# Where two query chunks are scaled, and where two keys' maxima and exponentials stand, in the first stage of an attention and Fourier-mixing kernel

## The chip, the cores and the metric

The kernel runs on one core of one Trainium2 chip. The time is device microseconds of one execution. Five engines work on their own instruction queues, each in program order: PE (TensorE: matrix products, and transposes done as products with an identity), DVE (VectorE), ACT (ScalarE), POOL (GpSimd) and SP (SyncE, which here only issues transfers). They wait for each other by semaphores. PE writes its results to an accumulator memory that DVE and ACT read.

## The reference

Eight batches of 576 tokens, eight heads of 64. The keys' softmax runs over the tokens, the queries' softmax over the 64 channels of a head:

```
q_s = exp(q - max(q, axis=-1));  q_s = q_s / (sum(q_s, axis=-1) + 1e-9)
k_s = exp(k - max(k, axis=2));   k_s = k_s / (sum(k_s, axis=2) + 1e-9)
kv  = einsum('bhsd,bhse->bhde', k_s, v)
x   = einsum('bhsd,bhde->bhse', q_s, kv)          # then (B, S, H*D)
u   = x + real(fft(fft(x, axis=1), axis=2))
un  = (u - mean(u)) / sqrt(var(u) + 1e-6)
out = u + relu(un @ w_ch1) @ w_ch2
```

A query row's softmax denominator is one number per token and head, and the product with kv is linear in the row. So a row may be divided before the product or the result after it.

## The kernel before

**Tiling.** Of a batch's 576 tokens 512 are worked on as four chunks of 128, named by (c, u) and below q00, q01, q10 and q11; the 64 others of two batches share one chunk (the "t" rows). The products x of a chunk land in a tile of its own, x00 to x11; c picks the half of a tile, u the tile. A batch has four key groups of 128 channels (two heads each).

**The stage in question** is the first batch, ahead of the first up-projection (`plain`, L876). The feed-forward part of batch after batch comes behind it and fills PE; the attention of the next batch is laid among those products. Only the first batch has no feed-forward to hide behind. In it, in order:

- *Keys.* `k_exp` (maximum, exponential with a running sum, reciprocal), `k_turn` (transposes on PE, copied to `ks` by ACT and, the fifth piece, DVE), `k_times_v` (product, scaled into the block-diagonal `kvr`).
- *Queries.* `q_exp` takes the maximum per head (L604, DVE), eight exponentials (L606, ACT), the sum, the added epsilon and the reciprocal (L608 to L610, DVE) and multiplies the chunk by it in place (L611, DVE). `q_turn` transposes it (L617, PE) and copies the result to `qT` (L624, ACT). `q_times_kv` multiplies by kvr (L649, PE) into an accumulator `acc` and copies it to x (L651, ACT). `acc` has three buffers, the transposes' `tr` has two, qT has two. `t_times_kv` does the same for the shared rows (L659, L665; copies L662 and L666).
- *Second batch's keys.* Their loads are at hand early. `second_keys` returns `maxima` and two lists of steps. `maxima` waits by a gate for their data and takes all four maxima (L468, DVE); a second gate, written behind x11, holds the first exponentials back until x is there. A gate is a one-row bit operation on DVE that reads one tile and rewrites another with its own value, so that what reads the second must wait for the first. `exps` does two exponentials (L475, ACT, with running sums) and two small DVE operations (L482, L483). The first two keys are exponentiated behind x, and transposed and multiplied between the folds and the Fourier blocks; the other two behind the first of the two mixes.
- *Transform.* `at_first` adds and subtracts the halves of x and folds columns (L688, L694, L703, L709, L710, all DVE); two of the column folds feed a product into scrap (`warm`, L206, PE), which writes nothing that is used. At its end a `wait_for` ties the first piece of weights (`convert(0)`: L351 and L356 on ACT, L352 and L353 on DVE, L357 on POOL) to the folds. Then five `block` steps: three products (L742, L745, PE) and three copies (L748, L751, L753, ACT) to Z.
- *Mixes.* `mix_own` twice: products (`second`, L766, L769), a copy to `sn` (L773, ACT), two combinations (L780, DVE), additions to x (L787, L788, DVE). Behind the first sn stands a gate on the second pair of maxima (L494).
- *Norm.* Statistics (L815, L816, DVE), root (L819, ACT), reciprocal (L820), the normalized rows (L832, DVE, order 0, 2, 1, 3), their transposes (L846, PE), the copies to `unT` (L850, ACT); with `unT` complete L876 begins. An unused `root` operation in `exps` (L481) has ACT load the table of the square root ahead of L819.

**Order.** The steps are listed by hand (L1098): `one` is the first batch's attention, `two` its folds, five blocks and two mixes, `some` and `others` the second batch's key steps. A scheduler then places the instructions of neighbouring steps on each engine; on the chip each engine runs its list in that order.

Of the kernel before, what the change touches and what calls it, by code (L numbers as in the profile page):

```python
# [40 lines left out]
F32 = mybir.dt.float32  # L41
I32, U32 = mybir.dt.int32, mybir.dt.uint32
ACT = mybir.ActivationFunctionType
ALU = mybir.AluOpType
AX = mybir.AxisListType

P = 128
B, H, S, DH = 8, 8, 576, 64
D = H * DH
FF = 4 * D  # L50
NR = H // 2
NC = 5
HD = D // 2
NN = HD + 1
# [43 lines left out]
def pipelined(items, stages):  # L98


    def step(t):
        for s in range(len(stages) - 1, -1, -1):
            if 0 <= t - s < len(items):
                stages[s](items[t - s])

    return [lambda t=t: step(t) for t in range(len(items) + len(stages) - 1)]
# [8 lines left out]
def interleaved(t):  # L115

    return t.rearrange("p (a q) -> p q a", a=2)


def paired(t):  # L120
    return t.rearrange("p (q a) -> p q a", a=2)


class _Block:
# [63 lines left out]
    def turned(self):  # L188
        t = self.ps.tile([P, 4, P], F32, tag="tr", name="tr", bufs=2)
        return t  # L190
# [264 lines left out]
    def second_keys(self):  # L455


        nc, V = self.nc, self.nc.vector
        items = [("k", 1, r) for r in range(NR)]
        m, rec = (self.small.tile([P, NR], F32, tag=n, name=n, bufs=1) for n in ("km1", "krec1"))  # L460

        self.km1 = m

        def maxima():
            self.gate(self.at_start[2][0][:, 1, :], self.second_at[0][0:1, ::S])
            for it in items:
                self.k_load(it)
                V.reduce_max(m[:, it[2]:it[2] + 1], self.live[it][0], axis=AX.X, negate=True)  # L468

            self.gate(self.xpart(0, 1, 1), m[0:1, 0:2])  # L470

        def exps(some):
            for it in some:
                k, i = self.live[it][0], slice(it[2], it[2] + 1)
                nc.scalar.activation(k, k, ACT.Exp, bias=m[:, i], accum_out=rec[:, i])  # L475
                self.live[it].append(rec[:, i])
            i = slice(some[0][2], some[-1][2] + 1)
            if some[-1] == items[-1]:

                t = self.small.tile([P, 1], F32, tag="root", name="root", bufs=1)  # L480
                nc.scalar.activation(t[:], rec[:, NR - 1:], ACT.Sqrt)  # L481
            V.tensor_scalar(out=rec[:, i], in0=rec[:, i], scalar1=ATT_EPS, scalar2=None, op0=ALU.add)  # L482
            V.reciprocal(rec[:, i], rec[:, i])  # L483

        turned = lambda some: pipelined(some, [self.k_turn, self.k_times_v])
        return maxima, [lambda: exps(items[:2])] + turned(items[:2]), [lambda: exps(items[2:])] + turned(items[2:])

    def gate(self, t, raw):
# [109 lines left out]
    def q_exp(self, it):  # L598
        nc, V = self.nc, self.nc.vector
        q = self.live[it][0]  # L600
        heads = q.rearrange("p (h d) -> p h d", h=H)
        spread = lambda t: t[:].unsqueeze(2).to_broadcast([P, H, DH])
        m = self.small.tile([P, H], F32, tag="qm", name="qm", bufs=3)
        V.reduce_max(m[:], heads, axis=AX.X, negate=True)  # L604
        for h in range(H):
            nc.scalar.activation(heads[:, h, :], heads[:, h, :], ACT.Exp, bias=m[:, h:h + 1])  # L606
        rec = self.small.tile([P, H], F32, tag="qrec", name="qrec", bufs=3)
        V.reduce_sum(rec[:], heads, axis=AX.X)  # L608
        V.tensor_scalar(out=rec[:], in0=rec[:], scalar1=ATT_EPS, scalar2=None, op0=ALU.add)
        V.reciprocal(rec[:], rec[:])  # L610
        V.tensor_tensor(out=heads, in0=heads, in1=spread(rec), op=ALU.mult)  # L611

    def turned_q(self, it):
        q = self.live.pop(it)[0]
        pt = self.turned()
        for r in range(NR):
            self.nc.tensor.transpose(pt[:, r, :], q[:, r * P:(r + 1) * P], self.ident[:])  # L617
        return pt

    def q_turn(self, it):  # L620
        _, b, c, u = it
        pt = self.turned_q(it)
        qT = self.work.tile([P, NR, P], F32, tag="qT", name="qT", bufs=2)
        self.nc.scalar.copy(qT[:], pt[:] if c == u else pt[:, :, ::-1])  # L624
        self.live[it] = qT

    def t_turn(self, it):
        pt = self.turned_q(it)
        self.tq = self.work.tile([P, NR, P], F32, tag="tq", name="tq", bufs=1)
        self.nc.scalar.copy(self.tq[:], pt[:])  # L630

# [11 lines left out]

    def q_times_kv(self, it):
        nc, (_, b, c, u) = self.nc, it
        qT = self.live.pop(it)
        px = self.acc((P, D))
        for r in range(NR):
            nc.tensor.matmul(px[:, r * P:(r + 1) * P], lhsT=qT[:, r, :], rhs=self.kvr[b % 2][:, r, :], start=True,  # L649
                             stop=True)  # L650
        nc.scalar.copy(self.xpart(b, c, u), px)  # L651

    def t_times_kv(self, b):
        nc, V = self.nc, self.nc.vector
# [20 lines left out]
    def transform(self, b):  # L675


        nc, V, G = self.nc, self.nc.vector, self.nc.gpsimd
        Z = self.work.tile([P, KT, HD], F32, tag="Z", name="Z", bufs=1)
        self.Z[b] = Z  # L680
        x = {(c, u): self.xpart(b, c, u) for c in range(2) for u in range(2)}
        eo = {}
# [34 lines left out]
        def at_first():  # L717

            for some in ((2, 3), (0, 1)):
                for f in (tokens_folded, columns_folded, by_frequency, columns_again):  # L720
                    f(some)

            self.wait_for(eo[1][:, NN:], [self.raws[0]])

        def block(k):

# [32 lines left out]
    def second(self, z, zr, add):  # L759

        nc, V = self.nc, self.nc.vector
        pm = self.acc((P, D))
        cd, n = self.cd, 0
        for k, at, size in ((1, 0, QD), (0, QD, QD + 1), (3, NN, QD - 1), (2, NN + QD - 1, QD)):
            rows = QD - 1 if k == 3 else P
            nc.tensor.matmul(pm[:, at:at + size], lhsT=z(k)[0:rows], rhs=cd[0:rows, at:at + size], start=True,  # L766
                             stop=(k != 0))
            if k == 0:
                nc.tensor.matmul(pm[:, at:at + size], lhsT=zr, rhs=cd[:, D:], start=False, stop=True)  # L769

        sn = self.sn[self.turns % 2]
        self.turns += 1
        nc.scalar.copy(paired(sn[:, 0:HD]), interleaved(pm[:, HD:]))  # L773
        if self.turns == 1:

            self.gate(sn[:], self.km1[0:1, 2:4])
        two = self.halves()
        a = interleaved(pm[:, 0:2 * (QD + 1)])[:, 0:QD, :]
        for i, op in enumerate((ALU.subtract, ALU.add)):
            V.tensor_tensor(out=paired(two[:, i * NN + 1:(i + 1) * NN]), in0=a, in1=paired(sn[:, 1:NN]), op=op)  # L780
        V.tensor_copy(two[:, ::NN], pm[:, QD:QD + 1].to_broadcast([P, 2]))
        add(two[:, 0:NN], two[:, NN:])
# [260 lines left out]
def kernel(ctx: ExitStack, tc: tile.TileContext, q, kT, v, w1, w2, ft,  # L1043
# [4 lines left out]
    def front(b, loads=None):  # L1048

        first = blk.attention(b, loads)  # L1050
        steps = late(lambda: blk.transform(b), (6, 9, 10)[min(b, 2)])
        mixes = [lambda c=c: blk.mix_own(b, c) for c in range(2)]
        if b % 2:

            mixes.insert(0 if b == B - 1 else 2, lambda: blk.mix_shared(b // 2))
        return first, steps + mixes

    def late(make, n):

        box = []  # L1060

        def run(i):
            if not box:
                box.extend(make())
            box[i]()

        return [lambda i=i: run(i) for i in range(n)]
# [3 lines left out]
    def norm(g):  # L1071
        def make():
            nexts[g], steps = blk.norm(g)
            return steps
        return late(make, 7)
# [19 lines left out]
    free = blk.hold()  # L1095
    one, two = front(0)
    maxima, some, others = blk.second_keys()
    for step in one + [maxima] + some[:1] + two[:1] + some[1:] + two[1:-1] + others[:1] + two[-1:] + others[1:] + norm(0):  # L1098
        step()

    groups = [*range(B - 1), B, B - 1]
    for order, g in enumerate(groups):
        loads = [] if g == 0 else None
        one, two = front(order + 1, loads) if order + 1 < B else (blk.later, [])
# [101 lines left out]
```

## Time and profile before

| what | us |
|---|---|
| median of 4 runs | 1129.68 (1128.59 to 1133.9) |
| the profiled execution | 1127.47 |
| its span, first to last instruction | 1125.6 |
| PE busy | 1091.7 |
| DVE, ACT, POOL busy | 542.7, 404.7, 333.9 |
| first up-projection product (L876) starts | 62.11 |

The span leaves out what lies around the instructions, 1.87 us in this execution. A row of the timeline has the start, the duration, the engine, the line of the kernel, the operation, what it writes and reads, and in brackets how long the engine was idle before it and whom it waited for. An "x2" row merges neighbouring instructions of one kind; the time from one start to the next can be shorter than the duration, since instructions of an engine overlap at their ends. Rows of PE's and of DVE's busy time count an engine as busy while an instruction is in it.

### The profile page before, as it was taken

Reading aid. Unit: us, or ns where it says so; the run is one execution under the profiler, and the core shown is the slowest. Engines: PE = TensorE matmul, PEld = TensorE weight load, DVE = VectorE, ACT = ScalarE, POOL = GpSimd, SP = SyncE. Lnnn points to the kernel's source line nnn. Section 1 sums busy time; section 2 is a strip of 40 time slices with the busy share of each in tenths; the row PEclk is TensorE's granted clock in tenths of the full one; section 3 lists DMA queues with packets and bytes.
Section 4 is the critical chain, followed back from the end, with each engine's and each line's share of the span. In section 5 each row is a group of like instructions: output and inputs, shape, how many; then the busy total and the mean of one; then the engine's idle time right before and its main releaser. Section 6 shows DMA issues by size and latency. Waiting matters only on the chain.

```text
span 1125.6 us, 14593 instructions
## 1 busy us (share of the span) xinstructions
PE 1091.7 (97%) x5440; PEld 915.7 (81%) x5440; DVE 542.7 (48%) x1117; ACT 404.7 (36%) x975; POOL 333.9 (30%) x304
## 2 busy tenths in 40 slices
PE   5799999999999999999999999999999999999997
PEld 5644456888888888898889888888889888888886
DVE  6784795478334733484434643683334252103301
ACT  6695424264224413361325232532333152201200
POOL 2064671244022510333023402351035203402320
PEclk9999999999999999999999999999999999999999
DMA  9566685454266424663455436543453443434451
GB/s 311 171 219 190 242 314 193 148 213 169 103 192 200 175 108 145 202 221 116 153 178 188 151 126 204 195 156 112 149 184 150 143 147 140 187 140 157 152 187 56
DMA packets 92582, 193.79 MB, mean 172 GB/s; under 512 B 23121, under 2 KB 59729, under 8 KB 85345
## 3 DMA queue, kind: packets, MB, share of 16 engines
q1 hardware_dynamic: 90712, 191.82, 49.6%
q10 hardware_dynamic: 1800, 1.05, 0.3%
q8 instruction: 43, 0.70, 0.3%
q14 instruction: 27, 0.21, 0.1%
HBM read 168.72 MB, written 28.31 MB: 175 GB/s over the span
## 4 chain that ended last, share of the span: by engine, by line
PE 85%; DVE 1%; POOL 1%; ACT 1%; issue 1%; ACTq 0%; POOLq 0%
PE bb L946 15%; PE bb L984 15%; PE ba L946 10%; PE bc L984 10%; PE bc L946 10%; PE ba L984 10%; PE acc L567 2%; PE acc L649 2%; PE bc L885 2%; PE acc L766 1%; PE acc L742 1%; PE acc L745 1%; PE tr L846 1%; PE tr L617 1%; PE tr L553 1%
## 5 line engine op out<-in xcount | busy, mean ns | idle before, releaser
L946 PE MATMUL bb<-unT,big 128*128 128x256 f32 x768 | 187.4, 381 | 0.0
L984 PE MATMUL bb<-big 128*128 128x256 f32 x768 | 172.1, 379 | 0.0
L946 PEld LDWEIGHTS bb<-unT,big 128*128 128x128 f32 x768 | 142.8, 190 | 23.6 <-DVE u L914 2.6
L984 PEld LDWEIGHTS bb<-big 128*128 128x128 f32 x768 | 145.4, 190 | 20.3
L363 POOL TENSOR_TENSOR big<-big 128x512 f32<-128x512 f32 (+1 forms) x38 | 46.2, 1216 | 306.9 <-ACT big L958 306.0
L958 ACT ACTIVATE big<-big 128x512 f32<-128x512 f32 x96 | 60.3, 629 | 182.6 <-DVE big L957 182.1
L946 PE MATMUL bc<-unT,big 128*128 128x256 f32 x512 | 125.4, 379 | 0.0
L946 PE MATMUL ba<-unT,big 128*128 128x256 f32 x512 | 123.6, 379 | 0.2 <-ACT unT L850 0.2
L984 PE MATMUL bc<-big 128*128 128x256 f32 x512 | 116.0, 379 | 0.5 <-DVE x L1001 0.5
L984 PE MATMUL ba<-big 128*128 128x256 f32 x512 | 114.8, 379 | 0.0
L918 DVE TENSOR_TENSOR u<-bb,s 128x512 f32<-128x512 f32 x40 | 27.6, 691 | 178.5 <-PE bb L984 120.8
L984 PEld LDWEIGHTS bc<-big 128*128 128x128 f32 x512 | 96.1, 190 | 14.3 <-DVE x L1001 0.9
L984 PEld LDWEIGHTS ba<-big 128*128 128x128 f32 x512 | 95.7, 190 | 12.1
L946 PEld LDWEIGHTS bc<-unT,big 128*128 128x128 f32 x512 | 95.1, 190 | 12.7
L946 PEld LDWEIGHTS ba<-unT,big 128*128 128x128 f32 x512 | 95.1, 190 | 12.2 <-ACT unT L850 0.5
L371 POOL TENSOR_TENSOR unT<-unT 128x512 f32<-128x512 f32 x8 | 14.2, 1773 | 182.4 <-DVE unT L370 182.4
L606 ACT ACTIVATE q<-q,qm 128x64 f32<-128x64 f32 x240 | 61.9, 340 | 5.7 <-DVE qm L604 5.4
L914 DVE TENSOR_TENSOR u<-bb,s 128x512 f32<-128x512 f32 x40 | 27.6, 691 | 72.9 <-PE bb L946 38.7
L957 DVE TENSOR_TENSOR big<-bc,u 128x512 f32<-128x512 f32 x64 | 44.1, 690 | 22.8 <-PE bc L946 21.7
L996 POOL TENSOR_TENSOR x<-x,u 128x512 f32<-128x512 f32 x14 | 17.7, 1266 | 113.9 <-DVE u L918 101.7
L850 ACT COPY unT<-tr 128x512 f32<-128x512 f32 x36 | 20.7, 586 | 79.4 <-PE tr L846 78.8
L957 DVE TENSOR_TENSOR big<-bb,s 128x512 f32<-128x512 f32 x32 | 22.1, 691 | 55.8 <-PE bb L946 55.8
(253 smaller groups left out, 1651.6 us busy)
## 6 DMA issues: line engine op xcount, KB each, us to landing
big<-w1s SPq DMA_DIRECT2D x64, 896.0 KB
big<-w2s SPq DMA_DIRECT2D x56, 1024.0 KB
big<-in_w_dram SPq DMA_DIRECT2D x21, 512.0 KB
q<-in_q_dram SPq DMA_DIRECT2D x27, 256.0 KB
k<-in_kT_dram SPq DMA_DIRECT2D x24, 288.0 KB
v<-in_v_dram SPq DMA_DIRECT2D x24, 256.0 KB
words<-in_w_dram SPq DMA_DIRECT2D x8, 512.0 KB
mirror<-x SPq DMA_DIRECT2D x14, 256.0 KB
```

The source lines that it names most:

```text
L363: e1.tensor_tensor(out=to(4), in0=at(2), in1=at(3), op=ALU.add)
L567: nc.tensor.matmul(pk, lhsT=ks[:, c, :], rhs=v[:, c, :], start=(c == 0), stop=(c == NC - 1))
L606: nc.scalar.activation(heads[:, h, :], heads[:, h, :], ACT.Exp, bias=m[:, h:h + 1])
L649: nc.tensor.matmul(px[:, r * P:(r + 1) * P], lhsT=qT[:, r, :], rhs=self.kvr[b % 2][:, r, :], start=True, stop=True)
L850: nc.scalar.copy(unT[:, u:u + 3:2, :, cols], pt[:].rearrange("p (a k) t -> p a k t", a=2))
L885: nc.tensor.matmul(po[:], lhsT=h[:, f, i * P:(i + 1) * P], rhs=self.w2sb[:, f, :], start=(f == 0), stop=(f == NF - 1))
L914: V.tensor_tensor(out=temp("u2"), in0=box["bb"][:], in1=box["s1"][:], op=ALU.add)
L918: V.tensor_tensor(out=temp("u3"), in0=box["bb"][:], in1=box["s1"][:], op=ALU.add)
L946: nc.tensor.matmul(bank()[:, i, :], lhsT=w[:, WA_AT[m], k * P:(k + 1) * P], rhs=unT[:, B_AT[m], k, :], start=first and i == 0 and k == 0, ...
L957: V.tensor_tensor(out=hp(i), in0=bank[:], in1=u[:], op=ALU.add)
L958: nc.scalar.activation(hp(i), hp(i), ACT.Relu)
L984: nc.tensor.matmul(bank()[:, i, :], lhsT=h[p][:, A_AT[m], i * P:(i + 1) * P], rhs=w[:, p, :], start=first and i == 0 and p == 0, stop=p == ...
```

## The change

Four edits. The denominators of q00 and q11 of the first batch are no longer multiplied into the chunk ahead of the transposes; they are kept, and DVE multiplies them in where it writes x00 and x11 out of the accumulator, in place of ACT's copy. The maxima of the third and fourth key of the second batch move out of `maxima` to the start of the second `exps`, behind a gate on the last fold; the wait that ties the first piece of weights to the folds now ties it to these maxima. The second `exps` step moves from between the two mixes to between the folds and the Z blocks. The gate behind the first sn goes, and the unused square root moves behind the second sn.

```diff
         def maxima():
             self.gate(self.at_start[2][0][:, 1, :], self.second_at[0][0:1, ::S])
             for it in items:
                 self.k_load(it)
+            for it in items[:2]:
                 V.reduce_max(m[:, it[2]:it[2] + 1], self.live[it][0], axis=AX.X, negate=True)
 
             self.gate(self.xpart(0, 1, 1), m[0:1, 0:2])
 
         def exps(some):
+            if some[-1] == items[-1]:
+
+                self.gate(self.folded, self.second_at[0][0:1, 2 * S::S])
+                for it in some:
+                    V.reduce_max(m[:, it[2]:it[2] + 1], self.live[it][0], axis=AX.X, negate=True)
+
+                self.wait_for(m[:, 2:4], [self.raws[0]])
             for it in some:
                 k, i = self.live[it][0], slice(it[2], it[2] + 1)
                 nc.scalar.activation(k, k, ACT.Exp, bias=m[:, i], accum_out=rec[:, i])
                 self.live[it].append(rec[:, i])
             i = slice(some[0][2], some[-1][2] + 1)
-            if some[-1] == items[-1]:
-
-                t = self.small.tile([P, 1], F32, tag="root", name="root", bufs=1)
-                nc.scalar.activation(t[:], rec[:, NR - 1:], ACT.Sqrt)
...
-        rec = self.small.tile([P, H], F32, tag="qrec", name="qrec", bufs=3)
+        rec = self.small.tile([P, H], F32, tag="qrec", name="qrec", bufs=4)
         V.reduce_sum(rec[:], heads, axis=AX.X)
         V.tensor_scalar(out=rec[:], in0=rec[:], scalar1=ATT_EPS, scalar2=None, op0=ALU.add)
         V.reciprocal(rec[:], rec[:])
+        if it[:2] == ("q", 0) and it[2] == it[3]:
+
+
+            self.live[it].append(spread(rec))
+            return
         V.tensor_tensor(out=heads, in0=heads, in1=spread(rec), op=ALU.mult)
...
-        qT = self.live.pop(it)
+        qT, *rec = self.live.pop(it)
         px = self.acc((P, D))
...
-        nc.scalar.copy(self.xpart(b, c, u), px)
+        x = self.xpart(b, c, u)
+        if rec:
+            heads = lambda a: a.rearrange("p (h d) -> p h d", h=H)
+            nc.vector.tensor_tensor(out=heads(x), in0=heads(px), in1=rec[0], op=ALU.mult)
+            return
+        nc.scalar.copy(x, px)
...
-            self.wait_for(eo[1][:, NN:], [self.raws[0]])
+            self.folded = eo[1][:, NN:]
...
-        if self.turns == 1:
-
-            self.gate(sn[:], self.km1[0:1, 2:4])
+        if self.turns == 2:
+
+            t = self.small.tile([P, 1], F32, tag="root", name="root", bufs=1)
+            nc.scalar.activation(t[:], sn[:, 0:1], ACT.Sqrt, scale=0.0)
...
-    for step in one + [maxima] + some[:1] + two[:1] + some[1:] + two[1:-1] + others[:1] + two[-1:] + others[1:] + norm(0):
+    for step in one + [maxima] + some[:1] + two[:1] + some[1:] + others[:1] + two[1:] + others[1:] + norm(0):
         step()
```

## The prediction

> **What bounds it now.** First the busy shares and the last chain on the page:
> ```profile
> PE 1091.7 (97%) x5440; PEld 915.7 (81%) x5440; DVE 542.7 (48%) x1117; ACT 404.7 (36%) x975; POOL 333.9 (30%) x304
> PE 85%; DVE 1%; POOL 1%; ACT 1%; issue 1%; ACTq 0%; POOLq 0%
> ```
> PE is the bound. The timeline of PE shows it full from the first up-projection (L876, 62.11 us) on, with one stall of 4.13 us at 139.3 to 143.4. The change touches only what lies ahead of 62.11; instruction orders after that are the same. So the forecast is the shift of that 62.11. The chain view names no piece before 126.92, so I follow the start in the timeline (start, duration, engine, idle before). First where the x rows are made:
> ```profile
> 28.40 0.69 DVE L611 TENSOR_TENSOR big<-big,qrec 128x512 f32<-128x512 f32 x1
> 29.24 0.63 PE L617 MATMUL tr<-ident,big 128*128 128x128 f32 x4
> 29.96 0.59 ACT L624 COPY qT<-tr 128x512 f32<-128x512 f32 x1 [1.46 <-PE tr L617]
> 30.44 0.58 ACT L666 COPY xs<-acc 64x512 f32<-64x512 f32 x1
> 30.92 1.07 ACT L651 COPY x<-acc 128x512 f32<-128x512 f32 x2
> 31.07 2.05 PE L649 MATMUL acc<-kvr,qT 128*128 128x128 f32 x16 [1.20 <-ACT xs L666]
> 32.02 0.69 DVE L688 TENSOR_TENSOR eo<-x 128x512 f32<-128x512 f32 x1
> 33.78 0.15 DVE L494 SCALAR_TENSOR_TENSOR km<-x,km 1x2 int32<-1x2 int32 x1 [0.61 <-ACT x L651]
> ```
> One thread: scaling q11, its transposes, two ACT copies, two products, x11, the gate, the next fold at 33.85. Then the end of the stage:
> ```profile
> 45.93 0.37 ACT L748 COPY Z<-acc 128x256 f32<-128x256 f32 x1 [0.43 <-PE acc L745]
> 48.35 0.37 ACT L773 COPY sn<-acc 128x256 f32<-128x256 f32 x1 [0.87 <-PE acc L766]
> 50.47 0.35 ACT L773 COPY sn<-acc 128x256 f32<-128x256 f32 x1
> 52.24 0.57 ACT L554 COPY ks<-tr 128x512 f32<-128x512 f32 x1
> 55.75 2.22 PE L567 MATMUL acc<-big,ks 128*128 128x128 f32 x10 [0.46 <-ACT ks L554]
> 56.34 0.17 DVE L820 RECIPROCAL std<-std 128x2 f32<-128x2 f32 x1 [0.45 <-ACT std L819]
> 58.67 0.59 ACT L850 COPY unT<-tr 128x512 f32<-128x512 f32 x1
> ```
> ACT waits for PE in the Z blocks; behind sn it is late itself: the second sn follows two exponentials, then a table load (50.83, 1.28), then ks. PE is slow in one stretch (PE busy, ..., clock):
> ```profile
> 34.10:37.50 3.40, 1.96 (x11) 1.29 (x9) 3.40 (x11) 1.80 (x5) 0.00 (x0) 1.00 1.10 348
> 50.70:54.10 3.40, 1.24 (x11) 1.24 (x12) 3.40 (x13) 2.34 (x5) 0.00 (x0) 1.00 0.02 5
> 54.10:57.50 3.40, 2.94 (x15) 2.54 (x14) 2.92 (x12) 2.06 (x6) 0.00 (x0) 0.50 0.00 0
> ```
>
> **The sum, step by step** (new orders of each engine read from the changed program; spacings of starts from the timeline).
>
> 1. *q00 unscaled.* Its multiply (0.68) goes and its transposes stand earlier, but on VectorE the chain of q01 behind it (sum L608 at 22.46 for 0.63, add 0.17, reciprocal 0.20, multiply 0.68) now has nothing between its links, each waiting for the one before plus about 0.05 to 0.1: multiply at 23.65, kvr of the fourth key (L575) at 24.25 for 23.81. PE's t product needs that kvr, so what the earlier transposes win is spent there: ACT copies the transposed q01 at 27.3 as before (27.35). Nothing.
>
> 2. *q11 unscaled.* Its transposes wait no longer for 28.40 + 0.69. Next late is PE's own product of q01, which stands before them (27.92, next start 0.93 later): they start near 28.85 for 29.24, **-0.39**. So qT at 28.85 + 0.72 = 29.57, xs + 0.48 = 30.05, product of q10 + 0.63 = 30.68 (offsets from the rows above). The second batch's gate now passes near 27.3, not 29.12. DMA moved 304 GB/s over 0 to 24 us, 7.3 MB; the loads issued up to the fourth second-batch key add up to 7.2 MB, so I cost it nothing; a wait to 29.1 would cost 0.6.
>
> 3. *x by other hands.* VectorE writes x00 and x11. x00 costs nothing: its 0.7 falls at 29.8 to 30.5, while VectorE has only the fold to wait for. Behind xs ACT's order was x00, x01, x10, x11; it is now x10, x01. So x01 sits behind x10, which waits for its product: 30.68 + 1.19 (31.07 to 32.26) = 31.87, then x01 32.35 to 32.94. The first fold needs x01: 32.97 for 32.02. Queued behind it on VectorE: scaling of x11 (+0.60), column fold (+0.60), gate (+0.35), second fold (+0.08), each number the spacing of such starts in the timeline: 34.60 for 33.85, **+0.75**, step 2 included. ScalarE's exponentials and PE's warming products (L206) wait for these. The read of acc moves from ACT (L651, 0.59) to VectorE. The page's row L957, acc-side operand and all, says 690 ns, L611 0.68. [...]
>
> 4. *Two maxima out of 29.31 to 32.04.* 1.37 less on VectorE, beside ACT and PE work that ends later: nothing. From 33.85 to the first Z block (41.69) the thread is fold, L206, transposes, ks copy, product, twice: all +0.75, 42.44.
>
> 5. *Maxima and exponentials before Z.* Folds end at 40.08 + 0.75 = 40.83; gate and two maxima (0.66 apart) take VectorE to 42.5; it had 1.25 idle there, and waits later for sn: free. ACT: exponential 41.85 (0.28 late for its maximum), kvr, exponential 43.31, Z copies from 44.10, 0.36 behind; the two weight pieces L351 and L356 (0.6 each) now stand among them. The fourth Z copy ends 47.3; PE reaches the first mix product at 47.45 anyway. Cover left: about 0.1. Cost taken 0; without any cover 2 x 0.77 + 0.28 = 1.8. POOL's L357 and SP's one word fetch behind it move from 44.4 to about 49; SP's next entry waited until 62.88: nothing.
>
> 6. *Tail.* First sn 49.10. The second no longer follows exponentials: 49.97. Table load, root, ks: + 0.36 + 1.41 = 51.74 for 52.24. Product +0.62, last transposes 53.58. PE's idle gap before the third key's product is now 1.9, not 2.23, and a 3.4 us window there holds about half, nearer to 1.96 of 3.40 (clock stayed 1.00) than to 1.24 (fell to 0.50). So full clock: ks of the fourth key 54.32 for 55.12, product 54.95 to 56.33 (1.38, as at 52.86, not 2.22). std is ready at 55.56 and VectorE's 0.45 wait goes; so do the gate and two small operations (0.22). un0 comes at 56.75 as before, but its transposes no longer stand behind the key's product, nor unT behind kvr (58.01): unT 58.0 for 58.67. The second std now stands behind kvr in ACT's queue: 56.95, un2 57.35 for 57.28, covered by L351. All follows: L351 58.6 (59.28), the other three copies, L356 among them, at the old spacings, up-projection at 62.11 - 0.67 = 61.44. From sn (49.10 for 48.35): **-1.42**.
>
> Sum: +0.75 - 1.42 = -0.67 us. Span 1124.9; with 1.87 around it (1127.47 - 1125.6), 1126.8. The profiled execution lies 2.2 under the median 1129.68, so the median becomes **1129.0**.
>
> [...] Cold again, product 2.22 and the second std behind it, the up-projection starts near 62.25.
>
> **Rivals.**
> - *Half clock stays* (23%): +0.15, 1129.8, slower than before. For it: PE still idles about 1.9 us. Place: fourth key's product ahead of std and un2; it decides once kvr ends 0.67 later than 57.0.
> - *ACT bounds the Z blocks* (14%): cover of 0.1 against two extra exponentials; if ten copies each start 0.1 later, +0.9: sum +0.25, up to +1.1 with no cover: 1129.9 to 1130.8. Against: ACT now idles 0.43 before each Z copy.
> - *The stall at 143.4 goes* (8%): its 4.1 on top, 1124.9. Its chain is POOL's L371 at 132.51, 5.6 idle, for a store of s issued at 127.78. It hangs on PE's own progress, so should move along whole.
> - *It grows* (12%): the same store, started 0.67 earlier, falls in behind another transfer and POOL waits its 5.6 twice: +5.6 - 0.67, 1134.6. No row speaks for it; it decides once L371 starts more than 8 us after L357 in place of 5.6.
> - Forecast 43%. That x is not scaled by VectorE cannot be: its instructions are in the program.
>
> **Chances.** Within 0.3% (3.4 us, about what a measurement of this kernel tells from no change): 0.43 + 0.23 + 0.14 = 0.80; faster 0.08; slower 0.12. Range: the three inner cases span 1129.0 to 1130.8, a whole loss of step 6 or of step 3 would move them by 1.4 down or up, and the four runs shown lie up to 1.1 under their median and, but for one, 0.4 over it: 1126.3 to 1132.3, with the last two rivals left out.
>
> **What would show it.** x10 ahead of x01 on ACT and the second fold near 34.6; first Z block near 42.4; fourth Z copy ended before PE is free; second sn near 50.0; clock 1.00 about 54 to 57; first L876 near 61.44. Wrong if the fold comes before 33.9, if Z is late against PE, or if L876 has moved by over 1.5.

## The result, and the profile after

| | before | after |
|---|---|---|
| median, us | 1129.63 (63 runs, 1127.12 to 1133.9) | 1128.59 (44 runs, 1126.73 to 1130.89) |
| ratio after to before | | 0.9986, 95% interval 0.998 to 0.9991 |
| the profiled execution, its span | 1127.47, 1125.6 | 1128.2, 1126.4 |
| first up-projection starts in it | 62.11 | 62.93 |

The changed kernel is about 1.6 us faster by the ratio (0.14%; the interval runs from 1.0 to 2.3 us), 1.0 by the medians. Yet the one profiled execution of the changed kernel is *longer* than the one of the kernel before. Both are right, and why is the main thing to learn here.

The page of the changed kernel has PE full as before, and the same work:

```profile
PE 1091.4 (97%) x5440; PEld 914.9 (81%) x5440; DVE 543.0 (48%) x1117; ACT 403.4 (36%) x973; POOL 333.9 (30%) x304
PE 86%; issue 1%; ACT 1%; DVE 0%; POOL 0%; ACTq 0%; POOLq 0%
```

Lines have moved: L642 is now L650, L617 is L624, L624 is L631, L651 is L664 (and L662 where VectorE writes x), L649 is L657, L688 is L701, L494 is L496, L742 is L754, L773 is L785, L567 is L569, L876 is L889. The timeline of the changed kernel where x is made (start, duration, engine, line, idle before):

```profile
29.18 0.60 PE L624 MATMUL tr<-ident,big 128*128 128x128 f32 x4
...
30.36 0.58 ACT L679 COPY xs<-acc 64x512 f32<-64x512 f32 x1
...
30.99 1.16 PE L657 MATMUL acc<-kvr,qT 128*128 128x128 f32 x8 [1.21 <-ACT xs L679]
32.18 1.07 ACT L664 COPY x<-acc 128x512 f32<-128x512 f32 x2 [1.25 <-PE acc L657]
32.82 1.16 PE L657 MATMUL acc<-kvr,qT 128*128 128x128 f32 x8 [0.68 <-ACT x L664]
33.29 0.69 DVE L701 TENSOR_TENSOR eo<-x 128x512 f32<-128x512 f32 x1 [2.66 <-ACT x L664]
34.02 0.69 DVE L662 TENSOR_TENSOR x<-acc,qrec 128x512 f32<-128x512 f32 x1
...
34.96 0.14 DVE L496 SCALAR_TENSOR_TENSOR km<-x,km 1x2 int32<-1x2 int32 x1
```

ScalarE copies x10 and x01 in one go at 32.18, and waits 1.25 us for x10's product first; x01 has long been ready. VectorE idles 2.66 us for it. PE in turn waits 0.68 us, since the q11 product needs an accumulator that one of these copies frees. The end of the stage in the same timeline:

```profile
47.08 0.44 ACT L760 COPY Z<-acc 128x256 f32<-128x256 f32 x1
...
47.81 0.83 PE L778 MATMUL acc<-cd,Z 128*128 128x128 f32 x6
...
49.45 0.37 ACT L785 COPY sn<-acc 128x256 f32<-128x256 f32 x1 [0.87 <-PE acc L778]
...
50.35 0.37 ACT L785 COPY sn<-acc 128x256 f32<-128x256 f32 x1 [0.52 <-PE acc L778]
...
52.14 0.57 ACT L556 COPY ks<-tr 128x512 f32<-128x512 f32 x1
...
52.76 2.40 PE L569 MATMUL acc<-big,ks 128*128 128x128 f32 x10 [1.91 <-ACT ks L556]
...
57.28 0.17 DVE L833 RECIPROCAL std<-std 128x2 f32<-128x2 f32 x1 [1.06 <-ACT std L832]
...
62.93 0.67 PE L889 MATMUL ba<-unT,big 128*128 128x512 f32 x1 [1.07 <-ACT unT L863]
```

The second sn waits for PE and no longer stands behind exponentials, as meant. But the product of the third key took 2.40 us, where 1.38 is its time at full clock. The table by stretches (us, busy time and count of PE, weight loads, DVE, ACT, POOL, then the clock) says why:

```profile
50.70:54.10 3.40, 1.49 (x8) 1.34 (x7) 3.40 (x11) 2.24 (x5) 0.00 (x0) 0.82 0.32 125
54.10:57.50 3.40, 2.94 (x17) 2.54 (x17) 2.34 (x8) 1.76 (x5) 0.00 (x0) 0.67 0.00 0
```

A stretch of half clock, which in the first profile of the kernel before lay over the fourth key's product, lies over the third key's here. That takes back in this execution most of what the shorter queue brought.

### The profile page after: what moved, and what is told of

It reads as the page before. It is cut to its first block, busy times and chain, and to the rows that moved or that the text cites. A ratio compares the mean times of both kernels' runs of the same rounds, so it can differ in the third digit from the quotient of the medians.

```text
span 1126.4 us, 14588 instructions
## 1 busy us (share of the span) xinstructions
PE 1091.4 (97%) x5440; PEld 914.9 (81%) x5440; DVE 543.0 (48%) x1117; ACT 403.4 (36%) x973; POOL 333.9 (30%) x304
## 4 chain that ended last, share of the span: by engine, by line
PE 86%; issue 1%; ACT 1%; DVE 0%; POOL 0%; ACTq 0%; POOLq 0%
PE bb L959 15%; PE bb L997 15%; PE ba L959 10%; PE bc L997 10%; PE bc L959 10%; PE ba L997 10%; PE acc L569 2%; PE acc L657 2%; PE bc L898 2%; PE acc L754 2%; PE acc L757 2%; PE acc L778 1%; PE tr L859 1%; PE tr L624 1%; PE tr L555 1%; PE ba L898 1%
```

## The experiments

The time is cut at four marks. The first is VectorE's L642, part of the shared rows' work and ahead of everything that the change moves; it began between 20.07 and 21.03 us in the executions below, and from it on this varying start drops out. (The q11 transposes would not do as a first mark, since the scaling moves them.) The second is the first product of the first Z block, the third the first sn, the last the up-projection. The first two marks before, then in the whole change:

```profile
20.07 0.75 DVE L642 TENSOR_TENSOR F<-T 128x272 f32<-128x272 f32 x1
...
41.80 0.66 PE L742 MATMUL acc<-ft,eo 128*128 128x144 f32 x4
```

```profile
20.18 0.76 DVE L650 TENSOR_TENSOR F<-T 128x272 f32<-128x272 f32 x1
...
42.91 0.66 PE L754 MATMUL acc<-ft,eo 128*128 128x144 f32 x4
```

All from the timelines of one profiled execution each:

| kernel | L642 to first Z block | Z block to first sn | first sn to up-projection | ratio to before (95%) | mean clock over its runs |
|---|---|---|---|---|---|
| before | 21.73 | 6.55 | 13.76 | | 0.9943 |
| before, second profile | 21.73 | 6.54 | 14.06 | | |
| whole change | 22.73 | 6.54 | 13.48 | 0.9986 (0.998 to 0.9991) | 0.9960 |
| scaling alone | 22.74 | 6.54 | 14.93 | 1.0009 (1.0001 to 1.0016) | 0.9937 |
| keys alone | 21.73 | 6.54 | 12.26 | 0.9982 (0.9975 to 0.9989) | 0.9961 |
| keys, q11 scaled in x | 21.77 | 6.54 | 12.26 | 0.9982 (0.9974 to 0.9989) | 0.9958 |
| keys, q00 scaled in x | 22.83 | 6.54 | 13.29 | 0.9989 (0.9979 to 0.9999) | 0.9950 |
| whole change, tail filled | 24.72 | 6.55 | 12.25 | 0.9986 (0.9979 to 0.9993) | 0.9959 |
| before, tail filled | 21.73 | 6.54 | 13.01 | 0.9980 (0.9973 to 0.9988) | 0.9968 |
| keys alone, tail and folds filled | 22.60 | 6.54 | 12.26 | 0.9983 (0.9977 to 0.999) | 0.9968 |

### The two halves of the change apart

**Scaling alone.** The keys' steps, gates and the square root stand as before (in part; against the changed kernel):

```diff
-            for it in items[:2]:
+            for it in items:
                 V.reduce_max(m[:, it[2]:it[2] + 1], self.live[it][0], axis=AX.X, negate=True)
...
-    for step in one + [maxima] + some[:1] + two[:1] + some[1:] + others[:1] + two[1:] + others[1:] + norm(0):
+    for step in one + [maxima] + some[:1] + two[:1] + some[1:] + two[1:-1] + others[:1] + two[-1:] + others[1:] + norm(0):
```

> Only q00 and q11 scaled in x; the keys' steps as before. Theory (copy order): ACT copies x10 ahead of x01, so the second fold starts about 1.1 us later than in the kernel before (34.9 to 35.0 for 33.85), nothing is won back, and the first up-projection product starts near 63.2 for 62.11: about 1 us slower, ratio near 1.001. Rival (the scaling is what makes the change faster): second fold at or before 33.8, ratio near 0.999.

Measured: 1130.77, ratio 1.0009 (1.0001 to 1.0016), slower by about 1 us. ScalarE's row for x in this kernel and PE's next product:

```profile
32.72 1.07 ACT L660 COPY x<-acc 128x512 f32<-128x512 f32 x2 [1.25 <-PE acc L653]
33.36 1.16 PE L653 MATMUL acc<-kvr,qT 128*128 128x128 f32 x8 [0.68 <-ACT x L660]
```

The same order, the same two waits, 22.74 us to the first Z block for 22.73. So this loss of 1.00 us belongs to the scaling. The up-projection came at 64.92 for the expected 63.2, since two stretches of half clock followed each other in the tail of this execution.

**Keys alone.** The scaling in x is switched off:

```diff
-        if it[:2] == ("q", 0) and it[2] == it[3]:
+        if False:
```

> Only the keys' maxima and exponentials moved; all chunks scaled ahead of their transposes. Theory: second fold at 33.85 as before, first Z block near 41.8, and the tail's gain (second sn and third ks no longer behind two exponentials) comes in whole: up-projection between 60.7 (full clock) and 61.9 (half clock), 1.3 to 2.5 us faster than before, ratio 0.9978 to 0.9988, better than the whole change by about 1 us. Rival (scaling makes the gain, the keys' move only shifts work): ratio 0.9995 to 1.0005.

Measured: 1127.57, ratio 0.9982 (0.9975 to 0.9989). From the first sn to the up-projection it took 12.26 us:

```profile
48.81 0.37 ACT L785 COPY sn<-acc 128x256 f32<-128x256 f32 x1 [0.87 <-PE acc L778]
...
61.07 3.24 PE L889 MATMUL ba<-unT,big 128*128 128x512 f32 x7 [1.02 <-ACT unT L863]
```

The tail ran at full clock, although TensorE stood idle 1.91 us ahead of the third key's product, exactly as in the whole change. So the wait alone does not decide on half clock.

The granted clock in the traces shows what does. In six profiled executions half clock came both in the first stage and at a stall near 140 us (see below), and the second time began 26, 27 or 33 times 3.413 us after the first (before: 54.13 and 142.88, 26 times 3.4134). So each execution has a grid of stretches of 3.413 us, at whose lines the clock changes; it lies elsewhere in each execution, in the two profiles of the kernel before 0.95 us apart as counted from L642. Here is the stretch with the wait in it, cut along the execution's own grid, in the whole change and then in the keys alone (whose grid is read from its half clock near 140 us):

```profile
49.48:52.90 3.42, 1.51 (x14) 1.28 (x13) 3.04 (x11) 2.84 (x6) 0.00 (x0) 1.00 0.45 153
52.90:56.31 3.41, 3.33 (x15) 2.92 (x15) 3.32 (x9) 0.97 (x4) 0.00 (x0) 0.50 0.00 0
```

```profile
50.41:53.82 3.41, 1.70 (x15) 1.69 (x15) 3.41 (x12) 2.19 (x5) 0.00 (x0) 1.00 0.24 95
53.82:57.24 3.42, 1.82 (x15) 1.43 (x13) 3.06 (x12) 2.40 (x8) 0.00 (x0) 1.00 0.00 0
```

The same wait leaves TensorE busy for 1.51 us of its stretch in one and 1.70 in the other. The ten executions of the table, cut in this way from 14 to 150 us, have 378 stretches at full clock. Half clock followed 16 of them, with TensorE busy for 0 to 1.57 us; the other 362 had 1.60 us or more. So the place of the wait on the grid decided.

**Which chunk costs.** One chunk at a time, the rest of the change as it is. First q11:

```diff
-        if it[:2] == ("q", 0) and it[2] == it[3]:
+        if it == ("q", 0, 1, 1):
```

> The whole change, but only q11 scaled in x; q00 scaled ahead of its transposes. Theory: ACT's order is again x00, x01, x10, so the first fold comes near 32.0 and the second near 33.5 to 33.9; otherwise as with the keys alone: up-projection between 60.5 and 61.8, ratio 0.9976 to 0.9988. Rival (the loss of the first stage lies in the scaling by VectorE itself, not in ACT's order): second fold near 34.9 as in the whole change, ratio 0.9986 as that.

Measured: 1127.84, ratio 0.9982 (0.9974 to 0.9989), 0.04 us more than the keys alone up to the first Z block and nothing in the ratio. Then q00, with `("q", 0, 0, 0)` in its place:

> The whole change, but only the chunk q00 is scaled in x; q11 is scaled ahead of its transposes as before. ScalarE's order of copies is x10, x01, x11 here. Theory A (the loss of the scaling is x01 standing behind x10 on ScalarE): the second fold lies 5.5 us or more behind the start of the q11 transposes, as with both chunks (5.78), not 4.8 as with q11 alone; ratio 0.9983 to 0.9992. Theory B (the loss is VectorE's writing of x, by the number of chunks that it writes): one chunk costs no more than the other, second fold 4.6 to 5.0 behind, ratio 0.9978 to 0.9984, as with q11 alone.

Measured: 1128.95, ratio 0.9989 (0.9979 to 0.9999). The gate ahead of the second fold comes 5.48 us behind the q11 transposes, the fold 5.56. So q00 carries the loss, +1.10 us to the first Z block, and q11 almost none. The reason is in ScalarE's list: with x00 gone to VectorE, ScalarE's list runs x10, x01, x11; with only x11 gone it is x00, x01, x10, and x01 waits for nobody.

### Is the gain a shorter queue or a faster clock?

**The whole change with TensorE kept busy (tail filled).** Three products of 256 columns, whose result nobody reads, between the transposes of the third key and its product:

```diff
+    def busy(self, n):
+
+        junk = self.acc((P, 512))
+        for _ in range(n):
+            self.nc.tensor.matmul(junk[:, 0:256], lhsT=self.ident[:], rhs=self.ft[:, 0:256], start=True, stop=True)
...
-    for step in one + [maxima] + some[:1] + two[:1] + some[1:] + others[:1] + two[1:] + others[1:] + norm(0):
+    for step in one + [maxima] + some[:1] + two[:1] + some[1:] + others[:1] + two[1:] + others[1:2] + [lambda: blk.busy(3)] + others[2:] + norm(0):
```

> The whole change, and three products of 256 columns into a free accumulator between the transposes and the product of the third key, where PE idles for 1.9 us; they write nothing that is used. Theory (half clock in the tail is an idle PE's): clock 1.00 from 50 to 58, product of the third key 1.4 instead of 2.4 us, up-projection near 62.0 for 62.93, about 0.5 to 0.9 us faster than the whole change, ratio to the kernel before near 0.998, and less spread between executions. Rival (the clock falls whatever PE does, or the products push the key's product back): clock still 0.5 somewhere, up-projection at 62.9 or later, ratio 0.9986 or above.

Measured: 1128.73, ratio 0.9986 (0.9979 to 0.9993): nothing gained. The tail did as expected: 12.25 us from the first sn, clock 1.00. But in the profiled execution half clock fell elsewhere, on the folds:

```profile
30.70:34.10 3.40, 2.41 (x15) 2.22 (x16) 0.69 (x1) 1.33 (x3) 0.00 (x0) 0.88 1.10 349
34.10:37.50 3.40, 2.29 (x7) 1.57 (x6) 2.88 (x7) 1.63 (x4) 0.00 (x0) 0.50 1.10 348
```

There TensorE waits 0.68 us for an accumulator and 1.11 us for the fold, both waits of the scaling. On this execution's grid the stretch from 29.84 to 33.26 had TensorE busy for 1.57 us, and two at half clock followed it. The way to the first Z block took 24.72 us, two more than in the whole change.

**The kernel before with the same three products.** No step is moved. As the scheduler laid them, two of the three stand ahead of the third key's transposes and one behind:

> The kernel before, with three products of 256 columns on data that lie ready, whose result nobody reads, put on TensorE between the transposes of the third key and its product. Theory A (what the move of the keys gains is mostly TensorE's clock, which the idle time there costs in most executions): with the idle time filled the kernel before gets most of that gain without any move: ratio to before 0.9983 to 0.9990, a higher mean clock over its runs than the 0.9943 of before's runs, and in the profile the clock 1.00 between 50 and 58 us. Theory B (the gain comes from the second sn and the key copies no longer standing behind the exponentials): the products change nothing of that, ratio 0.9996 to 1.0004.

Measured: 1127.36, ratio 0.9980 (0.9973 to 0.9988). Its timeline in the tail:

```profile
48.79 0.37 ACT L779 COPY sn<-acc 128x256 f32<-128x256 f32 x1 [0.87 <-PE acc L772]
...
49.48 1.03 PE L206 MATMUL acc<-ft,ident 128*128 128x256 f32 x4
...
50.90 0.60 PE L206 MATMUL acc<-ft,ident 128*128 128x256 f32 x2
53.30 1.38 PE L573 MATMUL acc<-big,ks 128*128 128x128 f32 x10 [1.81 <-ACT ks L560]
...
56.02 1.38 PE L573 MATMUL acc<-big,ks 128*128 128x128 f32 x10 [0.79 <-ACT ks L560]
...
61.80 3.67 PE L882 MATMUL ba<-unT,big 128*128 128x512 f32 x8 [0.95 <-ACT unT L856]
```

Both key products take 1.38 us, though 1.81 us of the wait is left: with the three products TensorE is busy for 1.60 us in the stretch of this execution's grid that holds it. The kernel before, with three unread products more and every other order as it was, reaches what the keys' move brings (theory A had expected a little less, 0.9983 to 0.9990). So theory A holds: most of the gain is clock. The queues' own part is the difference at full clock, 13.01 with everything in its old place against 12.26 with the keys moved: 0.75 us.

**The keys moved, tail and folds filled.** The three products, and four warming products for two in the folds (`self.warm(t[:, 0:HD], 4)`):

> Only the move of the keys (no scaling in x), with the same three products ahead of the third key's product, and four instead of two warming products for each fold in the stage at 33 to 37 us. Theory A (half clock after idle time is what is left between this and its best executions, 1126.0): mean clock of its runs above the 0.9961 of the keys' move alone, ratio to before 0.9972 to 0.9978, and fewer runs above 1128. Theory B (idle TensorE in these two places no longer costs clock once the keys are moved): ratio 0.9980 to 0.9985, as for the move alone, or worse if the warming products delay the transposes of the third key.

Measured: 1127.61, ratio 0.9983 (0.9977 to 0.999): theory B by the time. The mean clock did rise, to 0.9968, but the extra warming products delay the transposes of the second batch's first key by 0.95 us (37.96 for 37.01 in the keys alone), and the first Z block with them (22.60 us behind L642 in place of 21.73). The clock paid for the delay and no more.

### Why the profiled execution of before was not a typical one

**A second profile of the kernel before.**

> The kernel before, once more, for a second profiled execution. Theory A (the first profiled execution was a rare one with little half clock): this one lies near 1129.5, mean clock 0.993 to 0.995, and its window table shows half clock for 5 us or more ahead of the first up-projection, which starts 1 to 2.5 us later than 62.11. Theory B (the difference between the median and the first profile lies elsewhere in the program): the first up-projection is again at 62.1 within 0.3, and the added time is behind it.

Measured: 1130.12, span 1128.3, 2.7 longer than in the first profile. The first up-projection starts at 62.52, 0.41 later, so neither theory had it whole: most of the added time is behind it. It comes at the stall near 140 us, where PE waits 4.12 us for a copy of qT. First the first profile's stretches, then the second's:

```profile
142.40:145.80 3.40, 2.40 (x11) 2.41 (x12) 3.40 (x6) 3.40 (x8) 2.47 (x3) 0.57 0.19 73
145.80:149.20 3.40, 3.40 (x13) 1.96 (x12) 3.40 (x5) 0.88 (x2) 2.37 (x3) 0.93 0.80 316
```

```profile
142.40:145.80 3.40, 2.01 (x9) 2.01 (x10) 3.40 (x5) 3.40 (x7) 2.15 (x2) 0.50 0.30 117
145.80:149.20 3.40, 3.40 (x9) 1.92 (x8) 3.40 (x5) 1.28 (x3) 2.29 (x3) 0.55 0.68 267
```

PE is busy throughout the second stretch in both, but issues 13 products in the one and 9 in the other. From the clocks (a stretch wholly at half clock shows 0.50, so one less the clock, times two, times 3.4 us, summed) the half clock lasted 3.4 us in the first and 6.5 in these two stretches of the second, with 0.3 more ahead of them, where the clock was 0.95: one stretch or two.

**The stall filled.** Seven products that nobody reads, ahead of the one that waits there:

```diff
+        if (b, c, u) == (1, 1, 0):
+            self.warm(self.ft[:, 0:HD], 7)
         px = self.acc((P, D))
```

It was put into the keys' move, then into the keys' move with the tail filled, and into the kernel before and the whole change with the tail filled:

> Only the move of the keys, with seven products on data that lie ready, whose result nobody reads, put on TensorE ahead of the product at the stall near 140 us (idle 4.15 us there, for the copy of qT). Theory A (what is left above the best executions is whole stretches of 3.4 us at half clock that this stall brings, one or two by execution, 1.2 to 1.7 us each): the stall's stretch shows clock 1.00, mean clock of the runs 0.9975 or more (0.9961 for the move alone), ratio to before 0.9960 to 0.9972. Theory B (the half clock there costs nothing, as ScalarE is what is late in that stretch and TensorE catches up behind it): clock up as in A, ratio 0.9979 to 0.9985 as for the move alone.

> Only the move of the keys, with both fillings: three products ahead of the third key's product, and seven in the stall near 140 us. Theory A: fewest executions with half clock of all: mean clock 0.998 or more, spread of the runs under 2 us, ratio to before 0.9958 to 0.9970. Theory B (half clock is not what differs between executions): spread of 3 to 5 us as for the move alone, ratio 0.9979 to 0.9985.

> The kernel before, nothing moved, with the same two fillings. Both kernels then run at full clock, so the difference to the keys' move with the same fillings is what the move gains in the queues alone. Theory A (0.75 us: from the first sn to the up-projection 13.01 us at full clock in the filled kernel before, 12.26 with the keys moved): median 0.4 to 1.1 us above that of the keys' move with both fillings. Theory B (the move's whole gain is clock, and its earlier end is lost again at a later wait): within 0.3 us of it.

> The whole change, scaling in x included, with the same two fillings. Theory A (the scaling costs about 1 us of order on ScalarE, whatever the clock): median 0.7 to 1.3 us above the 1125.08 of the keys' move with both fillings, and so above the 1125.63 of the filled kernel before as well, that is 1125.8 to 1126.4; a run in which the wait for the folds near 33 to 37 us falls on a stretch of half clock lies 1 to 2 us higher. Theory B (the scaling costs clock alone): within 0.3 us of 1125.08, with the mean clock 0.999.

| kernel, with the stall filled | median, us | lowest to highest | mean clock | ratio to before (95%) |
|---|---|---|---|---|
| keys alone (5 runs) | 1125.79 | 1124.91 to 1127.7 | 0.9972 | 0.9963 (0.995 to 0.9975) |
| keys alone, tail filled (5 runs) | 1125.08 | 1124.52 to 1125.14 | 0.9990 | 0.9954 (0.994 to 0.9967) |
| before, tail filled (5 runs) | 1125.63 | 1125.19 to 1126.45 | 0.9996 | 0.9962 (0.9949 to 0.9974) |
| whole change, tail filled (12 runs) | 1127.55 | 1125.44 to 1129.99 | 0.9972 | 0.9973 (0.9963 to 0.9984) |

The timeline and the stretch at the stall in the second kernel of the table:

```profile
137.83 3.19 PE L212 MATMUL tr<-ft,ident 128*128 128x256 f32 x14
142.41 1.16 PE L665 MATMUL acc<-kvr,qT 128*128 128x128 f32 x8 [1.40 <-ACT qT L637]
```

```profile
142.40:145.80 3.40, 3.39 (x17) 2.39 (x18) 3.40 (x4) 3.20 (x6) 2.63 (x4) 1.00 0.09 35
```

The awaited product starts no earlier than the copy allows, but takes 1.16 us in place of 2.08 (1.93 in the profile of the keys alone), and what follows runs at full clock. The keys' move with both fillings reached 0.9954, a little more than theory A's 0.9958 to 0.9970, and with the stall alone filled 0.9963, inside its range, at a mean clock of 0.9972, just under the expected 0.9975. The version with both fillings is the fastest found: 4.9 us under the kernel before by the medians shown (1129.96 there), with its five runs within 0.6 us of each other. With the clock held, moving the keys is worth 0.55 us (1125.08 against 1125.63), near the 0.75 of the marks. The whole change lies 2.5 us above the keys alone (2.1 by the ratios; the kernel before, measured anew beside it, took 1130.1), where theory A had 0.7 to 1.3 and theory B under 0.3: both missed. Five of its twelve runs have a mean clock of 0.998 or more and took 1125.44 to 1126.62, with a median of 1125.64, as the filled kernel before. The other seven lie at 0.993 to 0.997 and 1127.26 to 1129.99. That this half clock is at the folds, as seen when TensorE was kept busy in the tail, is the likeliest reading, but not shown; no run with a lower clock was profiled here.

## Why the prediction was right, and where it was not

The forecast was 1129.0 for 1128.59, no difference that can be told, from a loss ahead of the Z blocks and a gain behind them. Both are there. Point by point:

- *The first Z block.* It came 22.73 us behind L642 for 21.73, +1.00 for the predicted +0.75. (The timeline's +1.11 has the stage's later start in it, 20.18 for 20.07. The prediction's 41.69 is the weight load of the first Z product; the product itself began at 41.80.)
- *q00 costs nothing (step 1).* Nearly so: ScalarE copied the transposed q01 at 27.55 for 27.35, 0.09 later with the start taken out.
- *q11's transposes 0.39 earlier (step 2).* This term was mis-sized: they came 9.00 us behind L642 for 9.17, 0.17 earlier. With q11 alone it was 0.25, for q01's product, which stands next, began 7.93 behind L642 as before, not earlier, and the transposes 0.99 behind that, not 0.93. The missing 0.22 is nearly all of what the Z block lost beyond the forecast; behind the transposes the prediction's own numbers make 13.70 us (with 0.11 added for the product), and 13.73 was measured.
- *x by other hands (step 3).* ScalarE's order was as read, and the page's row for VectorE out of an accumulator held (690 ns in L957): L662 took 0.69 us, as L701 does. PE's wait of 0.68 us for an accumulator was not foreseen. The q11 product ended at 33.98 by it, so x11's scaling began 0.73 behind the first fold, for 0.60 in the sum; it costs clock too, as the filled tail showed.
- *Maxima and exponentials ahead of Z (steps 4 and 5).* Right. The last full Z copy starts at 47.08 and PE's first mix product at 47.81, 1.11 behind its old time, as the first Z block is: no delay is added between (6.54 us for 6.55). The cover of 0.1 held.
- *The tail (step 6).* The size was right at full clock: 12.26 measured for 12.34 predicted, within 0.01 in every kernel with the keys moved whose tail ran at full clock. In the profiled execution of the change it was 13.48, since half clock stayed. The failing part is the sentence "So full clock": it took the clock as a property of the kernel, full after and half before. The share of a stretch was the right quantity (1.57 us fell, 1.60 stayed), but where the stretches lie differs between executions of one kernel: the same tail left 1.51 us in one and 1.70 in the other. The rival "half clock stays" and the forecast are both true, of different executions. The rival's size was short: it put half clock on the fourth key's product (13.15 us from sn), and here it lay on the third's.
- *The median 2.2 above the profiled execution.* That was carried over as a constant. As the second profile shows, what the first one was spared was a second stretch of half clock at the stall near 140 us, and 0.30 us in the tail: with the change the same difference is 0.4 (1128.59 against 1128.2).
- *The range.* Its terms add up to 1126.5 to 1132.6, not to 1126.3 to 1132.3; nothing hangs on it.

So why 1.6 us by the ratio, and not 0.67? The mean clock over the runs is 0.9943 before and 0.9960 after. 0.0017 of 1126 us is 1.9 us of lost clock, about one stretch (half of 3.4 us is 1.7). At the same mean clock of 0.995 the two kernels take the same time, 1129.16 before (34 runs) and 1129.28 after (12 runs). By the marks at full clock, too, the change is no gain: 22.73 + 12.26 against 21.73 + 13.01, +0.25 us. What the change brings, by these numbers, is less half clock: less in the tail, for which the keys' move stands, and some of it given back by the waits that the scaling puts ahead of the folds. So the forecast's order of effects was right, but that 1129.0 lies so near 1128.59 is in part luck: it counted one stretch of half clock in one execution, where the gain is a share of many.

That share can be estimated. A stretch of 3.413 us, slid along a profiled execution in steps of 0.1 us, has TensorE busy for under 1.6 us (the limit lies between the 1.57 and the 1.60 measured above) over 2.7 us of starts in the tail of the kernel before, over 1.6 with the keys moved, over none with three unread products in either; ahead of the folds over none before and 0.5 in the whole change. If the grid lies anywhere with equal chance, 79% of executions meet half clock in the tail before and 47% with the keys moved, and 15% of those of the whole change ahead of the folds. This is an estimate; of the runs without a profile only the mean clock is known. It does not explain all: in the whole change with both fillings seven of twelve runs had a lower clock.

Of the other rivals, neither happened. The stall near 140 us is 4.13 us long before and after. ScalarE did not bound the Z blocks.

## What to carry to other kernels

Where the last engine of a chain must hand a result on, look at the order on the engine that makes it: taking one of four copies away let a late one in ahead of an early one, and cost more than the copy. Before a gain of a microsecond is credited to an edit, compare its mean clock with that of the old kernel over many executions, and give the *old* kernel a few products that nobody reads in its idle place: if that gains as much, the edit was a way to keep TensorE busy. And mark out stages inside one execution, from a mark that the edit cannot move: the start of this stage moved by 1.0 us between executions (L642 at 20.07 to 21.03), more than most steps here are worth, and the q11 transposes, moved by the scaling, would have put the loss to the first Z block at 1.17 us for 1.00.

## What the runs showed of the hardware

In the first stage and at the stall near 140 us half clock came in whole stretches of 3.413 us (in the first profile of before from 54.13 to 57.54 us at 0.50, with 1.00 in the stretches on both sides) on a grid that lay elsewhere in each execution (half clock at 54.13 and 142.88 us in one, at 53.30 and 142.05 in another). In the 378 stretches at full clock between 14 and 150 us, with 1.57 us or less of TensorE's work in a stretch the next ran at half clock, with 1.60 or more it did not. A stretch at half clock was followed by another where TensorE was busy for up to 2.75 us of it (6 cases), and by full clock from 2.87 us on (16). In the first 14 us stretches with as little work brought no half clock (0.42 and 0.88 us from 2.93 and 6.34 us on in the first profile of before); why is open. So the same idle time of 1.91 us ahead of the same product brought half clock in the whole change and none in the keys alone, and the idle time of 4.1 us at the stall one stretch (first profiles of before and of the whole change) or two (second profile of before).

The clock decides the time to a degree that surprised: over 75 runs of the kernel before, with a mean clock of 0.995 the median is 1129.16 (34 runs), with 0.993 it is 1131.52 (15 runs), and the three with 0.990 or less lie between 1133.93 and 1135.3. Filling two waits with ten products that nobody reads took the median of the kernel before down by 4.3 us (ratio 0.9962, 0.9949 to 0.9974), with its five runs 1.3 us apart, in a kernel whose page shows TensorE 97% busy and a clock of 9 tenths in every slice.
